# Two blocks of 128 rows taken from the first half of batch 0, in a Fourier mixing and mixture-of-experts kernel

## The chip, the cores and the metric

The kernel runs on one core of one Trainium2 chip. The core has a matrix engine (TensorE, PE in the profile, with its weight loads as PEld), a vector engine (VectorE, DVE), a scalar engine (ScalarE, ACT), GpSimd (POOL), and SyncE (SP), which here only issues transfers. The metric is the device time of one execution in microseconds (us). The kernel before takes 1270.7 us, the median of 3 runs (1270.32 to 1275.03).

## The reference

The input `x` has 8 batches of 2496 rows of 256 values. Each batch goes through a two-dimensional Fourier transform, of which the real part is kept. The 19968 resulting rows are tokens for a layer of 8 experts: the largest of 8 logits chooses a token's expert.

```python
X = np.fft.fft(x, axis=1)
X = np.fft.fft(X, axis=2)
x = X.real                              # (8, 2496, 256) -> (19968, 256)
logits = x @ w_gate                     # 8 experts
expert_idx = np.argmax(logits, axis=1)
gate_w = softmax(logits)[arange(N), expert_idx]
for e in range(8):                      # the rows of expert e
    h = np.maximum(x_e @ w1[e], 0.0)    # 256 -> 1024
    y_e = h @ w2[e]                     # 1024 -> 256
out = gate_w[:, None] * y               # in the tokens' order
```

All arithmetic is in float32. No token is dropped, whatever the experts' loads are.

## The kernel before, in words

**The transform.** A batch is worked in two passes. `first(b)` loads three tiles `xq`, folds them on VectorE (L295 to L306), multiplies them (`s`, TensorE) and writes the result to `Td` in DRAM (L342). `regroup(b, h)` reads `Td` back in another layout into a tile `t4` (t<-Td, L354), one transfer for each half of the batch. `second(b)` makes two more products of it (`pr` and `p`): for each of the two halves h, five windows of 128 positions with two tokens each. A window ends in VectorE's copies into `lg` (the logits, L408) and `rows` (the tokens, L410). After five windows `route(b, h)` finds each token's expert and its place in `Xs`, a buffer in DRAM with one region for each expert, and advances `base`, the next free place of each region. It puts ten scatters (128 rows each) on the list `waiting`. `send()` issues one of them on GpSimd (L236, Xs<-rows,pi). So a batch takes twenty scatters, ten for each half.

**The plans.** `rounds()` says, for each batch, how many blocks of which size can be worked once that batch has been scattered, whatever the experts' loads: blocks that are certain to be full. `plan(b, size, k, last)` computes on VectorE which expert and which rows of `Xs` each of k blocks has, some two dozen small instructions on one partition (L488 to L521) in four stretches with a `yield` behind each. Its tables have MOST = 21 entries, whatever k is. The result lies in `tabs`. `gone` keeps the first row of each region that no plan has given away yet.

**The blocks.** `in_order()` lists all blocks. `experts(todo)` works them. For each block SyncE reads the table, fetches the rows (`fetch_rows`, L534 and L538, xb<-Xs) and the expert's two weight arrays (`fetch_weights`, L544 and L546, 1 MB each, three buffers each). VectorE turns the rows (`turn`, L582) and ScalarE negates half of them (L585); TensorE multiplies (`ph`), VectorE and ScalarE take the positive part (L827, L829), TensorE multiplies again (`py`), ScalarE scales by the gate (L881), and GpSimd scatters the result to the output. Blocks from batch 2's round on have 512 rows, and most use a scheme with seven products in place of eight.

**What sets the order.** Every engine works its instructions in the order in which the program issues them, and the program is written as generators that are stepped in turn. The loop over b at the end takes steps of `experts` for round b - 1 and, for a share of each, steps of `side`: the plans of the round (`close`), the passes of the batches that follow (`mixed`, `ahead_of`), and `send`. In the first round, `experts` waits until the table of its first block exists, asks for its weights, has all waiting scatters issued and waits until the batch counts as whole; then it fetches the rows, lets nine steps of other work go ahead, and turns the first block.

**Which fetch waits for which scatter.** `sent` and `taken` tell the tile framework that a fetch for a block of round b waits for the scatters of batches up to b and not for later ones. Batch 0's two halves have the same number b = 0 there, so the first fetch waits for all twenty scatters of batch 0. The framework has eight semaphores for SyncE's and ScalarE's transfers together, taken in turn: a transfer waits for the one eight places before it. GpSimd's scatters have eight of their own.

**The first round before.** Batch 0 gives two blocks of 256 rows and four of 128 (1024 rows); batch 1 gives four of 256.

Of the kernel before, what the change touches and what calls it, by code (L numbers as in the profile page):

```python
# [15 lines left out]
ALU = mybir.AluOpType  # L16
ACTF = mybir.ActivationFunctionType
AX_X = mybir.AxisListType.X
PSUM = bass.MemoryType.PSUM

B, S, D = 8, 2496, 256
NA, NB = 104, 24
# [9 lines left out]
HW = NW // 2  # L32
HALF = -(-NG // 2)
LAST = NW * 128 - (NG - 1) * GP
NT = B * S
E, F = 8, 1024
FC = F // 128
BIG, BLK, REST = 512, 256, 128
# [12 lines left out]
def bc(ap, axis, n):  # L51
    shape = list(ap.shape)
    shape.insert(axis, n)
    return ap[tuple([slice(None)] * axis + [None])].to_broadcast(shape)
# [72 lines left out]
    return {n: np.ascontiguousarray(v, dtype=np.float32) for n, v in c.items()}  # L127


def rounds():  # L130

    want = [((256, 2), (128, 4)), ((256, 4),)] + [((512, B),)] * (B - 2)
    plan, used = [], 0

    def full(done, size):
        return max(0, -(-(done - used - E * (size - 1)) // size))

    for b in range(B):  # L140
        done = (b + 1) * S
        now = []
        for size, most in want[b]:
            k = min(full(done, size), most)
            if k:
                now.append((size, k, False))
            used += size * k
        if b == B - 1:
            k = full(done, BLK)
            used += BLK * k  # L150
            now.append((BLK, k, False))
            now.append((REST, (NT - used + E * (REST - 1)) // REST, True))
        plan.append(now)
    return plan

SURE = -(-(NT - sum(size * k for now in rounds() for size, k, last in now if not last)) // REST)


def in_order():


    todo = []
    for b, now in enumerate(rounds()):
        parts = [[(b, size, last, i) for i in range(k)] for size, k, last in now]
        if b == B - 1:
            few, many = parts[-2:]
            sure, more = many[:SURE], many[SURE:]
            k = len(few)  # L170
            end = more[(len(more) + 1) // 2:]
            more = more[:len(more) - len(end)]
            rest = []
            for i in range(k):
                rest += few[i:i + 1] + sure[len(sure) * i // k:len(sure) * (i + 1) // k][:1]
                rest += more[i:i + 1]
                rest += sure[len(sure) * i // k:len(sure) * (i + 1) // k][1:]
            parts = parts[:-2] + [rest + end]
        todo += sum(parts, [])
    return todo  # L180
# [5 lines left out]
AHEAD = 12  # L186
WARM = 16
MOST = max(k for now in rounds() for _, k, _ in now)


def halved(b, size):

    return size == 512 and b > 2 or size == 256 and b == B - 1
# [22 lines left out]
def kernel(ctx: ExitStack, tc, x, w_gate, w1, w2, out):  # L216
    nc = tc.nc
    vec, act, pool = nc.vector, nc.scalar, nc.gpsimd
# [50 lines left out]
    con, k = {}, 0  # L269
# [91 lines left out]
    def second(b):  # L361

        t4 = None

        def turn_last(h):

            nonlocal t4
            t4 = ahead.pop((b, "t4", h))
            n = min(HALF, NG - h * HALF)
            pr = pm_.tile([GP, HALF], F32, tag="m", name="pr")  # L370
            mm(pr[:, 0:n], con["rot"][:], t4[0:GP, 0:n, H])
            act.copy(t4[0:GP, 0:n, H], pr[:, 0:n])

        def group(g):
            i, n = g % HALF, LAST if g == NG - 1 else GP
            p2 = pm_.tile([128, 2, n], F32, tag="m", name="p2")
            for c in range(2):
                mm(p2[:, c], t4[0:GP, i, c * H:(c + 1) * H], con["m2"][:, c, 0:n])
            act.copy(zz[:, :, g * GP:g * GP + n], p2[:])
            if g == HALF - 1:  # L380
                turn_last(1)

        def mirror(rows, k):
            act.copy(free(rows[:], (k + 1) * W + D - 1, [-W, 2], [-1, H - 1]),
                     free(rows[:], k * W + 1, [W, 2], [1, H - 1]))

        turn_last(0)
        yield
        group(0)
        yield  # L390
        group(1)
        yield
        for h in range(2):
            rows = sp.tile([128, NSL, W], F32, tag="rows", name="rows")
            lg = sp.tile([128, NSL, E], F32, tag="lg", name="lg")
            for i in range(HW):
                w, k = HW * h + i, 2 * i
                if w + 2 < NG:
                    group(w + 2)
                p3 = pm_.tile([128, 2 * NY + 2 * E + 1], F32, tag="m", name="p3")  # L400
                z = zz[:, :, 128 * w:128 * (w + 1)]
                mm(p3[:, 0:NY + 2 * E], z[:, 0], con["rd"][:, 0, 0:NY + 2 * E], True, False, skip_group_check=True)
                mm(p3[:, NY:], z[:, 1], con["rd"][:, 1], False, True, skip_group_check=True)
                zs = sp.tile([128, NY + 1], F32, tag="zs", name="zs")
                act.copy(zs[:], p3[:, NY + 2 * E:])  # L405
                if i:
                    mirror(rows, k - 2)
                vec.tensor_copy(lg[:, k:k + 2], p3[:, NY:NY + 2 * E].rearrange("p (m e) -> p m e", m=2))  # L408
                for m, op in enumerate((ALU.add, ALU.subtract)):
                    vec.scalar_tensor_tensor(rows[:, k + m, 0:NY], p3[:, 0:NY], zs[:, 0:1], zs[:, 1:],  # L410
                                             op0=ALU.add, op1=op)
                yield
            mirror(rows, k)
            yield from route(b, h, rows, lg)

    def route(b, h, rows, lg):
# [6 lines left out]
        mx, eq, v = small("mx", NSL), small("eq", NSL, E), small("v", NSL)  # L423
# [31 lines left out]
        vec.tensor_tensor(nxt[:], rk[:, NSL], base[:], op=ALU.add)  # L455
        base = nxt
        for s in range(NSL):
            waiting.append((b, pf[:, s:s + 1], pi[:, s:s + 1], rows[:, s]))

    waiting = deque()  # L460

    def send():

        if waiting:
            b, place, idx, rows = waiting.popleft()
            if b:
                due = sp.tile([128, 1], F32, tag="due", name="due", bufs=8)
                act.copy(due[:], place)  # L468
                pool.tensor_copy(idx, due[:])  # L469
            sent(put_row(Xs, idx, rows, E * CAP - 1, "xs"), b)  # L470
# [7 lines left out]
    def plan(b, size, k, last):  # L478
# [3 lines left out]
        def one(name, *dims, dt=F32):  # L482
            return cp.tile([1, *dims], dt, tag="p_" + name, name="p_" + name, bufs=2 if name == "gone" else 1)
# [10 lines left out]
        vec.tensor_tensor(ex[:], ce[:], nb[:], op=ALU.subtract)  # L494
        yield
        vec.scalar_tensor_tensor(rb[:], ex[:], -float(size), gone[:], op0=ALU.mult, op1=ALU.add)
        ge, ei = one("ge", MOST, E), one("ei", MOST)
        val, eq, rw = one("val", MOST, E + 1), one("eq", MOST, E + 1), one("rw", MOST)
        vec.tensor_tensor(ge[:], bc(bk["i"], 2, E), bc(ce[:], 1, MOST), op=ALU.is_ge)
        vec.reduce_sum(ei[:], ge[:], axis=AX_X)  # L500
        yield
        vec.tensor_tensor(eq[:], bc(ei[:], 2, E + 1), bc(bk["e9"], 1, MOST), op=ALU.is_equal)
        vec.memset(val[:, :, E:E + 1], float(E * CAP))
        vec.scalar_tensor_tensor(val[:, :, 0:E], bc(bk["i"], 2, E), float(size), bc(rb[:], 1, MOST),
                                 op0=ALU.mult, op1=ALU.add)
        yield
        vec.tensor_tensor(val[:], val[:], eq[:], op=ALU.mult)
        vec.reduce_sum(rw[:], val[:], axis=AX_X)
        tab = cp.tile([1, 2, MOST], I32, tag="p_tab", name="p_tab", bufs=4)
        vec.tensor_copy(tab[:, 0], rw[:])  # L510
        vec.tensor_scalar(tab[:, 1], ei[:], E - 1.0, None, op0=ALU.min)
        if last:
            cnt = cp.tile([1, 1], I32, name="cnt")
            vec.tensor_copy(cnt[:], ce[:, E - 1:E])
# [213 lines left out]
    def experts(todo):  # L728
# [35 lines left out]
        for k, (b, size, last, at) in enumerate(todo):  # L764
            n, m = size // 128, BIG // size
            if not k:
                while todo[0][:3] not in tabs:
                    yield 0, False
                fetch_some(0, 1)
                while b not in whole:  # L770
                    yield 0, True
                fetch_some(0)
                for _ in range(9):
                    yield 0, False
                for xT in turn(b, size, xbs[0][0]):
                    pass
# [129 lines left out]

    def close(b):

        for size, k, last in rounds()[b]:
            yield from plan(b, size, k, last)  # L910

    def through(b):
# [5 lines left out]
    def ahead_of(b):  # L918

        yield from first(b)  # L920
        regroup(b, 0)
        regroup(b, 1)
# [43 lines left out]
    for c in range(2):  # L966
# [6 lines left out]
            vec.tensor_scalar(con["rd"][:, c, to + E:to + 2 * E], pg[:], con["sgn"][:], None, op0=ALU.mult)  # L973
        else:
            vec.tensor_copy(con["rd"][:, c, to + E:to + 2 * E], pg[:])
    early = ahead_of(1)
    for _ in range(7):
        next(early)
    for k, _ in enumerate(second(0)):
# [5 lines left out]
    for b in range(1, B):  # L985
# [3 lines left out]
        ticks = TICKS + AHEAD * (b == 1)  # L989
        if b == 1:  # L990
            side = woven(chain(close(0), through(0)), chain(early, side))
        blocks = [(size, k * size / BIG, halved(b - 1, size)) for size, k, _ in rounds()[b - 1]]
        total = sum(k * (15 if seven_ else 16) for _, k, seven_ in blocks)
        open_ = sum(k * (8 if seven_ else 16) for _, k, seven_ in blocks)
        while done < total:
# [73 lines left out]
```

## Time and profile before

| | |
|---|---|
| median of 3 runs | 1270.7 us (1270.32 to 1275.03) |
| profiled execution | 1270.37 us, span 1268.5 us, mean TensorE clock 0.98 |
| TensorE | 1212.5 us busy (96% of the span), weight loads 1083.6 us |
| VectorE, ScalarE, GpSimd | 773.6, 421.5 and 445.7 us busy |
| DMA | 249.79 MB, mean 197 GB/s; SyncE's queue holds 49.9% of sixteen engines' span |
| weight transfers | 132 of 1 MB, 7.0 us from issue to landing (median) |
| rows for blocks | 112 transfers of 128 KB, 52 of 64 KB, 100 of 32 KB |

A line of the timeline gives the start, the duration, the engine, the line of the program, the operation, the tiles written and read (out<-in), the shapes, how many records, and in brackets the engine's idle time before it with what ended it. Most matrix products have line L221 and most GpSimd transfers L236, since helpers issue them; they are told apart by their tiles. A float32 product shows as two records. The page's line PEclk gives, for 40 equal slices of the span, the clock that TensorE was granted, in tenths. A line of the waits gives who waited for whom, the sum in us, how often, and the longest.

### The profile page before, as it was taken

What the parts mean: (1) busy time and instruction counts of PE and PEld (TensorE: products, weight loads), DVE (VectorE), ACT (ScalarE), POOL (GpSimd) and SP (SyncE); (2) the same over time, 40 slices, a digit from 0 to 9 for tenths busy, and PEclk for the clock granted to TensorE, in tenths of its full rate; (3) what the DMA queues carried; (4) which work ended last, traced back from release to release, by engine and by line L of the source; (5) the groups of instructions that cost most, each with busy time, mean ns of one, the idle gap of its engine ahead of it and who ended that gap; (6) DMA issues with size and microseconds to landing.
All of it is one profiled execution on the core that took longest, in us unless ns stands there. A gap on an engine that the chain in (4) does not pass through costs nothing.

```text
span 1268.5 us, 22212 instructions
## 1 busy us (share of the span) xinstructions
PE 1212.5 (96%) x7289; PEld 1083.6 (85%) x7289; DVE 773.6 (61%) x1884; ACT 421.5 (33%) x1087; POOL 445.7 (35%) x527
## 2 busy tenths in 40 slices
PE   5759999999999999999999999999999999999996
PEld 4548987876788899888998999889999999999995
DVE  4546334443465788576866588686788884444662
ACT  1423332332243433434243433432332322222222
POOL 0145427145116522472226612561462331111112
PEclk9869999999999999999999999999999999999997
DMA  8769898765348454573336435443444348777786
GB/s 239 246 194 334 306 311 305 193 223 176 124 151 254 139 148 154 165 249 114 101 127 207 136 117 171 133 153 96 146 130 159 104 157 288 278 284 270 270 292 231
DMA packets 163216, 249.79 MB, mean 197 GB/s; under 512 B 118601, under 2 KB 130227, under 8 KB 143516
## 3 DMA queue, kind: packets, MB, share of 16 engines
q1 hardware_dynamic: 146327, 203.28, 49.9%
q0 software_dynamic: 15888, 42.14, 9.2%
q10 hardware_dynamic: 885, 2.94, 0.7%
q8 instruction: 59, 0.97, 0.3%
q14 instruction: 57, 0.47, 0.1%
HBM read 194.91 MB, written 54.83 MB: 197 GB/s over the span
## 4 chain that ended last, share of the span: by engine, by line
PE 71%; issue 16%; DMA 4%; POOL 4%; DVE 3%; ACT 0%; POOLq 0%; SPq 0%; DVEq 0%; ACTq 0%
PE py L221 19%; PE a L221 10%; PE c L221 10%; PE d L221 7%; PE ph L221 6%; PE p L221 6%; PE b L221 5%; PE e L221 3%; PE s L221 3%; POOL out_dram L236 3%; DMA xq<-in_x_dram 1%; POOL Xs L236 1%; DMA t<-Td 1%; DMA w<-c_w 1%; DMA Xs<-rows,pi 0%
## 5 line engine op out<-in xcount | busy, mean ns | idle before, releaser
L236 POOL DMA_INDIRECT out_dram<-y,ro x163 | 161.0, 988 | 633.8 <-ACT y L678 297.9
L221 PE MATMUL py<-w_sb,hT 128*128 128x256 f32 x1504 | 340.3, 380 | 0.0
L221 PEld LDWEIGHTS py<-w_sb,hT 128*128 128x128 f32 x1504 | 282.0, 191 | 36.1 <-issue 1.0
L236 POOL DMA_INDIRECT Xs<-rows,pi x160 | 163.7, 1023 | 113.7 <-DVE rows L410 55.0
L221 PE MATMUL ph<-xT,w_sb 128*128 128x128 f32 (+2 forms) x992 | 173.0, 331 | 9.8 <-DVE ro L782 8.7
L221 PEld LDWEIGHTS ph<-xT,w_sb 128*128 128x128 f32 x992 | 137.7, 194 | 34.2 <-issue 16.5
L221 PE MATMUL a<-xT,w_sb 128*128 128x256 f32 (+1 forms) x512 | 118.1, 358 | 0.3 <-DVE xT L582 0.2
L827 DVE TENSOR_SCALAR hT<-ph 128x512 f32<-128x512 f32 x43 | 29.7, 690 | 127.7 <-PE ph L221 68.9
L585 ACT ACTIVATE xT<-xT 128x256 f32<-128x256 f32 (+1 forms) x94 | 36.5, 388 | 185.8 <-DVE xT L582 135.7
L221 PEld LDWEIGHTS a<-xT,w_sb 128*128 128x128 f32 x512 | 88.6, 191 | 10.6 <-DVE xT L582 1.3
L881 ACT ACTIVATE y<-py,xb 128x256 f32<-128x256 f32 x97 | 45.8, 473 | 154.4 <-PE py L221 152.6
L634 DVE TENSOR_TENSOR hT<-hT,b 128x512 f32<-128x512 f32 x57 | 39.2, 688 | 80.6 <-PE b L221 53.9
L408 DVE COPY lg<-p 128x16 f32<-128x16 f32 x80 | 13.8, 172 | 113.8 <-ACT zs L405 113.7
L644 ACT ACTIVATE hT<-a 128x512 f32<-128x512 f32 x57 | 34.0, 597 | 140.2 <-PE a L221 140.2
L221 PE MATMUL s<-xq,w 104*112 104x256 f32 (+2 forms) x208 | 61.5, 420 | 11.6 <-DVE xq L297 8.9
L582 DVE STREAM_TRANSPOSE xT<-xb 128x512 f32<-128x512 f32 (+1 forms) x94 | 58.7, 627 | 12.7 <-DMA xb<-Xs 12.7
L469 POOL CAST pi<-due 128x1 int32<-128x1 f32 x140 | 42.2, 301 | 68.8 <-ACT due L468 68.7
L221 PE MATMUL a<-w_sb,hT 128*128 128x128 f32 x528 | 66.0, 276 | 0.0
L221 PE MATMUL p<-table,zz 128*128 128x145 f32 (+1 forms) x320 | 58.3, 308 | 8.0 <-DVE rows L410 6.6
L221 PE MATMUL d<-w_sb,hT 128*128 128x128 f32 x528 | 65.5, 275 | 0.0
L221 PEld LDWEIGHTS a<-w_sb,hT 128*128 128x128 f32 x528 | 63.2, 192 | 0.7
L221 PEld LDWEIGHTS d<-w_sb,hT 128*128 128x128 f32 x528 | 62.2, 192 | 0.0
(144 smaller groups left out, 2086.0 us busy)
## 6 DMA issues: line engine op xcount, KB each, us to landing
w_sb<-in_moe_w_dram SPq DMA_DIRECT2D x132, 1024.0 KB, 7.0
xq<-in_x_dram SPq DMA_DIRECT2D x24, 896.0 KB, 8.6
xb<-Xs SPq DMA_DIRECT2D x112, 128.0 KB, 3.3
Td<-t SPq DMA_DIRECT2D x18, 448.0 KB, 3.3
t<-Td SPq DMA_DIRECT2D x8, 768.0 KB, 9.5
t<-Td SPq DMA_DIRECT2D x8, 640.0 KB, 9.2
xb<-Xs SPq DMA_DIRECT2D x52, 64.0 KB, 5.9
xb<-Xs SPq DMA_DIRECT2D x100, 32.0 KB, 5.4
```

What stands on the lines that cost most here:

```text
L221: nc.tensor.matmul(o, lhsT=lhsT, rhs=rhs, start=start, stop=stop, **kw)
L236: return unordered(pool.indirect_dma_start(out=dst, out_offset=bass.IndirectOffsetOnAxis(ap=idx, axis=0), in_=rows, in_offset=None, bounds ...
L408: vec.tensor_copy(lg[:, k:k + 2], p3[:, NY:NY + 2 * E].rearrange("p (m e) -> p m e", m=2))
L469: pool.tensor_copy(idx, due[:])
L582: vec.transpose(free(xT[:], 256 * h, [32, n // 32], [BIG, 2], [1, 32]), free(xb, 512 * h, [64, n // 32], [1, 2], [2, 32]))
L585: act.activation(odd, odd, ACTF.Copy, scale=-1.0)
L634: vec.tensor_tensor(h12, h11, b[:], op=add)
L644: act.activation(h11, a[:], ACTF.Relu)
L827: vec.tensor_scalar(o, ph[:], 0.0, None, op0=ALU.max)
L881: act.activation(y[:, i % 2], py[:], ACTF.Copy, scale=meta[:, i, 1:2])
```

## The change

Batch 0's first half gets a round of its own, with the number -1. Its 1256 tokens are certain to fill two blocks of 128 rows (`HEAD`). Their plan, `close(-1)`, is stepped in `second(0)` once in each window of the second half, so that it uses `base` as the first half leaves it. The first half's scatters are marked -1, so the fetch of these two blocks waits for the ten scatters of the first half alone. The remaining rounds take the rows given away into account: batch 0's own round then has one block of 256 and four of 128 (with the head 1024 rows again, in seven blocks in place of six). The tables of all plans are cut to the k entries that the plan needs. In `experts`, fifteen steps of other work go ahead of the first block's turning instead of nine.

```diff
--- before.py
+++ after.py
@@ -127,12 +127,15 @@
     return {n: np.ascontiguousarray(v, dtype=np.float32) for n, v in c.items()}
 
 
+HEAD = [(REST, -(-(2 * 128 * HW - NB - E * (REST - 1)) // REST), False)]
+
+
 def rounds():
 
 
 
     want = [((256, 2), (128, 4)), ((256, 4),)] + [((512, B),)] * (B - 2)
-    plan, used = [], 0
+    plan, used = [], sum(size * k for size, k, _ in HEAD)
 
     def full(done, size):
         return max(0, -(-(done - used - E * (size - 1)) // size))
@@ -154,15 +157,20 @@
     return plan
 
 
-
-SURE = -(-(NT - sum(size * k for now in rounds() for size, k, last in now if not last)) // REST)
+def stage(b):
+    return HEAD if b < 0 else rounds()[b]
+
+
+
+SURE = -(-(NT - sum(size * k for now in [HEAD, *rounds()] for size, k, last in now if not last)) // REST)
 
 
 def in_order():
 
 
     todo = []
-    for b, now in enumerate(rounds()):
+    for b in range(-1, B):
+        now = stage(b)
         parts = [[(b, size, last, i) for i in range(k)] for size, k, last in now]
         if b == B - 1:
             few, many = parts[-2:]
@@ -394,6 +402,8 @@
             rows = sp.tile([128, NSL, W], F32, tag="rows", name="rows")
             lg = sp.tile([128, NSL, E], F32, tag="lg", name="lg")
             for i in range(HW):
+                if h and not b:
+                    next(heads, None)
                 w, k = HW * h + i, 2 * i
                 if w + 2 < NG:
                     group(w + 2)
@@ -455,7 +465,7 @@
         vec.tensor_tensor(nxt[:], rk[:, NSL], base[:], op=ALU.add)
         base = nxt
         for s in range(NSL):
-            waiting.append((b, pf[:, s:s + 1], pi[:, s:s + 1], rows[:, s]))
+            waiting.append((b if b or h else -1, pf[:, s:s + 1], pi[:, s:s + 1], rows[:, s]))
 
     waiting = deque()
 
@@ -463,7 +473,7 @@
 
         if waiting:
             b, place, idx, rows = waiting.popleft()
-            if b:
+            if b > 0:
                 due = sp.tile([128, 1], F32, tag="due", name="due", bufs=8)
                 act.copy(due[:], place)
                 pool.tensor_copy(idx, due[:])
@@ -494,21 +504,22 @@
         vec.tensor_tensor(ex[:], ce[:], nb[:], op=ALU.subtract)
         yield
         vec.scalar_tensor_tensor(rb[:], ex[:], -float(size), gone[:], op0=ALU.mult, op1=ALU.add)
-        ge, ei = one("ge", MOST, E), one("ei", MOST)
-        val, eq, rw = one("val", MOST, E + 1), one("eq", MOST, E + 1), one("rw", MOST)
-        vec.tensor_tensor(ge[:], bc(bk["i"], 2, E), bc(ce[:], 1, MOST), op=ALU.is_ge)
-        vec.reduce_sum(ei[:], ge[:], axis=AX_X)
-        yield
-        vec.tensor_tensor(eq[:], bc(ei[:], 2, E + 1), bc(bk["e9"], 1, MOST), op=ALU.is_equal)
+        ge, val, eq = (one(name, MOST, E + 1)[:, 0:k] for name in ("ge", "val", "eq"))
+        ei, rw = (one(name, MOST)[:, 0:k] for name in ("ei", "rw"))
+        count = bk["i"][:, 0:k]
+        vec.tensor_tensor(ge[:, :, 0:E], bc(count, 2, E), bc(ce[:], 1, k), op=ALU.is_ge)
+        vec.reduce_sum(ei, ge[:, :, 0:E], axis=AX_X)
+        yield
+        vec.tensor_tensor(eq, bc(ei, 2, E + 1), bc(bk["e9"], 1, k), op=ALU.is_equal)
         vec.memset(val[:, :, E:E + 1], float(E * CAP))
-        vec.scalar_tensor_tensor(val[:, :, 0:E], bc(bk["i"], 2, E), float(size), bc(rb[:], 1, MOST),
+        vec.scalar_tensor_tensor(val[:, :, 0:E], bc(count, 2, E), float(size), bc(rb[:], 1, k),
                                  op0=ALU.mult, op1=ALU.add)
         yield
-        vec.tensor_tensor(val[:], val[:], eq[:], op=ALU.mult)
-        vec.reduce_sum(rw[:], val[:], axis=AX_X)
+        vec.tensor_tensor(val, val, eq, op=ALU.mult)
+        vec.reduce_sum(rw, val, axis=AX_X)
         tab = cp.tile([1, 2, MOST], I32, tag="p_tab", name="p_tab", bufs=4)
-        vec.tensor_copy(tab[:, 0], rw[:])
-        vec.tensor_scalar(tab[:, 1], ei[:], E - 1.0, None, op0=ALU.min)
+        vec.tensor_copy(tab[:, 0, 0:k], rw)
+        vec.tensor_scalar(tab[:, 1, 0:k], ei, E - 1.0, None, op0=ALU.min)
         if last:
             cnt = cp.tile([1, 1], I32, name="cnt")
             vec.tensor_copy(cnt[:], ce[:, E - 1:E])
@@ -770,7 +781,7 @@
                 while b not in whole:
                     yield 0, True
                 fetch_some(0)
-                for _ in range(9):
+                for _ in range(15):
                     yield 0, False
                 for xT in turn(b, size, xbs[0][0]):
                     pass
@@ -906,7 +917,7 @@
 
     def close(b):
 
-        for size, k, last in rounds()[b]:
+        for size, k, last in stage(b):
             yield from plan(b, size, k, last)
 
     def through(b):
@@ -973,7 +984,7 @@
             vec.tensor_scalar(con["rd"][:, c, to + E:to + 2 * E], pg[:], con["sgn"][:], None, op0=ALU.mult)
         else:
             vec.tensor_copy(con["rd"][:, c, to + E:to + 2 * E], pg[:])
-    early = ahead_of(1)
+    heads, early = close(-1), ahead_of(1)
     for _ in range(7):
         next(early)
     for k, _ in enumerate(second(0)):
@@ -989,7 +1000,7 @@
         ticks = TICKS + AHEAD * (b == 1)
         if b == 1:
             side = woven(chain(close(0), through(0)), chain(early, side))
-        blocks = [(size, k * size / BIG, halved(b - 1, size)) for size, k, _ in rounds()[b - 1]]
+        blocks = [(size, k * size / BIG, halved(b - 1, size)) for size, k, _ in (HEAD if b == 1 else []) + stage(b - 1)]
         total = sum(k * (15 if seven_ else 16) for _, k, seven_ in blocks)
         open_ = sum(k * (8 if seven_ else 16) for _, k, seven_ in blocks)
         while done < total:
```

## The prediction

> **What bounds the kernel now.** I read the busy shares first, then TensorE's waits, then the order of time around the one long wait, then DMA by stage.
>
> ```profile
> PE 1212.5 (96%) x7289; PEld 1083.6 (85%) x7289; DVE 773.6 (61%) x1884; ACT 421.5 (33%) x1087; POOL 445.7 (35%) x527
> PEclk9869999999999999999999999999999999999997
> ...
> PE ph L221 <- DVE ro L782: 8.7, 1, 8.7
> PE pr L221 <- DMA t<-Td: 2.8, 2, 2.4
> ```
>
> TensorE is busy 96% of 1268.5 us, so only its holes can be won. The waits of the first 130 us show one hole of 8.7 us: the first expert product `ph`. From 130 to 345 us the list has a single wait over 1 us, 3.2 us of `pr` on t<-Td. The chain of waits tells what the long hole consists of (start, us, what):
>
> ```profile
> 81.81 0.31 issue
> 82.12 2.42 DMA Xs<-rows,pi
> 84.79 0.35 SPq L534
> 86.39 1.92 DMA xb<-Xs
> 88.44 0.71 DVE xT L582
> 89.21 3.77 PE ph L221 x8
> ```
>
> The twentieth scatter of batch 0 lands at 84.5; only then are the rows fetched (84.79), turned (88.44) and multiplied (89.2). TensorE had nothing from 80.5:
>
> ```profile
> 77.94 1.21 PE L221 MATMUL p<-table,t 120*128 120x120 f32 x4 [0.20 <-DVE rows L410]
> 78.94 0.41 PE L221 MATMUL pr<-t,table 120*120 120x5 f32 x2
> 79.21 1.32 PE L221 MATMUL p<-table,zz 128*128 128x145 f32 x4
> 89.20 3.78 PE L221 MATMUL ph<-xT,w_sb 128*128 128x256 f32 x8 [8.67 <-DVE ro L782]
> ...
> 131.87 0.28 PE L221 MATMUL pr<-t,table 120*120 120x6 f32 x2
> ```
>
> The last line is the place where I expect the gain to be cut: batch 2's first product from `t`, which runs without a wait now. Its transfer landed 5 us before (issued 118.52, 8.3 us to landing: 126.8). DMA by stage (start:end, PE, PEld, DVE, ACT, POOL busy, clock, DMA share, GB/s):
>
> ```profile
> 60.00:80.00 20.00, 12.42 (x62) 10.69 (x62) 17.29 (x73) 5.28 (x17) 15.73 (x15) 0.69 0.77 271
> 80.00:90.00 10.00, 1.33 (x5) 0.89 (x4) 1.45 (x5) 0.99 (x3) 2.48 (x3) 0.50 0.32 81
> 90.00:110.00 20.00, 19.99 (x107) 17.25 (x106) 10.16 (x39) 7.42 (x23) 3.52 (x7) 0.87 0.92 301
> 110.00:130.00 20.00, 18.83 (x103) 16.29 (x102) 13.94 (x52) 6.96 (x30) 16.30 (x24) 1.00 1.01 326
> ```
>
> In the hole DMA idles too (0.32); right behind it DMA is full (0.92, 1.01). So two resources stand close together there.
>
> **The Trainium skill.** "TensorE: Matmul & The Clock Gate", "What's actually happening", says that the array falls to half clock after an idle window of about 3.4 us and is released after about as long of work. The trace agrees: clock 0.50 from 75 to 95 us, the first eight `ph` take 3.78 us where later ones take 1.89. "DMA: Bandwidth & Descriptors", "Queues, rings and completion order", says that one queue's descriptors are consumed in ring order on each DMA engine, and the queues are served in turn. The trace fits: rows issued at 94.6 behind a 0.9 MB `xq` took 10.0 us to land (1.9 us without it).
>
> **The change, part by part.**
>
> *Head plan (21 small DVE instructions, L488 to L521).* A plan takes 4.0 us in the trace (from 70.19: 1.4 + 0.7 + 0.5 + 1.4). At 2 entries instead of 21, six instructions fall from 0.32-0.34 to about 0.16 (the 1x8 rows): 3.0 us. The two plans of batch 0 shorten likewise, by 1.0 and 0.9. Net +1.1 us, against 1.8 us of DVE gaps between 54.5 and 59.6. DVE is full from 59.6 to 77.1; the first head block is turned behind the same work: at 77 to 78. POOL is covered: the second half's indices come up to 2 us later than 63.3, and POOL gets to them at 69.2. The other plans save about 9 us of DVE in all, off the path: nothing.
>
> *Head rows.* In the built program their fetch waits for exactly ten scatters. The tenth starts at 67.37; scatters land in 2.4 to 3.2 us here, 4.7 to 6.5 in full stretches: 70 to 73.5. First issue to data took 3.65 us (84.79 to 88.44): 74 to 77, just ahead of DVE. First `ph` at 78.0 (transposition 0.43, the copy into `ro`).
>
> *Fifteen steps.* They put the plans and folds on DVE ahead of the transposition. On TensorE only the `s` of 68.2 stands ahead of the first `ph` in the built order; two rounds of `p`, an `s` and a `pr` that run from 69.2 to 80.5 now come behind it. So TensorE will stand still from about 70 to 78, a hole of 7 to 9 us for DVE. It takes the place of two: 3.48 us at 71 (for `rows`) and the 8.67 us.
>
> *Two blocks of 128 for one of 256.* TensorE: 2 x 3.57 (32 records of 128x128) against 6.91, +0.23 us; `py` is the same 3.46 per 128 rows. One weight pair more, 2.1 MB, and this counts below.
>
> *TensorE up to `pr`.* From 69.17 to 131.87 are 62.7 us; less waits 3.48 + 8.67 + 1.17 + 0.4, and half clock 2.9 (74.7 to 80.5) and 3.0 (89.2 to 94.6), 43.1 us at full clock. Adding up the groups gives 41.5; I take 42.5, with the 0.23. The restart at 78 is cold once: 2.5; small waits 0.5. So `pr` is reached at 123.5 (121.5 to 125.5), 8.4 us earlier.
>
> *The queue on SP up to `pr`.* In the built order two things move: the weights of the second and third block stand ahead, and t<-Td of batch 2 stands behind the rows and weights of block (0,128,1), not before them. Each transfer also waits for the eighth before it, so t<-Td waits for the `xq` just before it. Prices from 99.8 to 126.8 us: 2.25 us per MB, rows of 256 2.0, rows of 128 1.2, a scatter or output 0.37. From 79.7: two weight pairs 9.4, Td and xq 3.1, rows 3.2, four scatters 1.5: 96.9. Then a weight pair, Td and xq 7.8; batch 1's scatters run beside it, one per 1.45 us, a quarter of the engines: 10.5, to 107.4. The last Td can't start before its `s`, about 109.5. Then Td and xq 3.1, rows 1.2, a weight pair 4.7, the first t<-Td 1.8: 10.8, with scatters 14.5, an output and first latency 2: 126. Five weight pairs stand ahead, three now; the idle 77 to 91 pays for most of it.
>
> *So `pr` waits* 126 - 123.5 = 2.5 us, which it doesn't now. Under about 3.4 us the clock holds; over it a restart costs 1.9 (after 3.15 us idle at 211, `p` took 1.19 for 0.6, `ph` x8 3.13 for 1.89). I take 0.5 of it. Sum: 126 + 0.5 - 131.87 = -5.4 us.
>
> *What is late next.* The weights of the following blocks are issued when buffers come free; (0,128,2)'s pair lands near 133 and is needed near 149. From there order and amounts on every engine are those of now, so the shift stays. The tail has the same count of blocks. Without DMA's idle stretch t<-Td would land 8 us later, and the change would lose.
>
> The profiled execution took 1270.4 (1268.5 and 1.9 around it), its neighbours 1270.3 to 1275.0, median 1270.7. 1270.4 - 5.4 = 1265.0.
>
> **Rivals.** *TensorE's whole lead stays:* if t<-Td lands before 123.5, 1270.4 - 8.4 = 1262. For it: single stretches of 5 us reach 404 GB/s, where my price is nearer 370. Against it: five weight pairs, and the late `s`. *Slower, through the same transfer:* from a landing at 130.0 on, the cold restart (1.9) makes it slower than now. For it: one `xq` took 12.1 us and one weight 11.1 in full stretches, and both stand ahead in series. At 134 it is 1274.5. Against it: the idle stretch is really free. *It doesn't do what it says:* the head's rows or its transposition come 8 us late, at 86, TensorE stands still until then with its `p` work queued behind, and 2.1 MB more follow: 1271 to 1277. Against it: ten counted scatters, and DVE's order.
>
> **How the numbers follow.** Forecast 0.52 (own range 1262.5 to 1269), the whole lead 0.25, slower through t<-Td 0.17, not doing what it says 0.06. About 0.5% (6.4 us) is what a measurement of this kernel can tell from no change. Faster, under 1264.3: 0.23 of the second case and 0.17 of the first, 0.40. Slower, over 1277: 0.05 and 0.03, 0.08. Same 0.52. The range 1259.5 to 1274.5 leaves out a tenth on each side.
>
> **What would show it.** Right: the first `ph` starts at 77 to 80 behind a wait of 7 to 9 us that DVE ends; a new wait of 1 to 5 us at the third `pr`, released by t<-Td, at 122 to 129; DMA share near 1 from 80 on; the same work behind it, about 5 us earlier. Wrong: first `ph` after 82 (then a late scatter or row fetch is named there), no wait at `pr` (the whole lead), or `pr` after 130.

## The result and the profile after

The changed kernel takes 1282.65 us (median of 11 runs, 1279.65 to 1292.63), the kernel before beside it 1273.59 us (11 runs, 1270.32 to 1279.32). The ratio is 1.0069, with a 95% interval of 1.0051 to 1.0087: slower, where 1265.0 us was forecast, 5.4 us under the profiled execution of the kernel before. The profiled execution of the changed kernel took 1284.77 us, its span is 1283.0 us. The two profiled executions lie 14.4 us apart, the two medians 9.1, so differences between these two traces are somewhat larger than the loss.

The page of the changed kernel first, the lines for busy time and for TensorE's clock in 40 slices:

```profile
PE 1215.7 (95%) x7321; PEld 1086.5 (85%) x7321; DVE 767.0 (60%) x1906; ACT 421.7 (33%) x1088; POOL 442.0 (34%) x527
PEclk9978899899999999999999999999999999999998
```

TensorE has 3.2 us more work than before and 14.5 us more span, so most of the loss is waiting. TensorE's waits of the first 160 us (us in all, times, longest):

```profile
PE pr L229 <- DMA t<-Td: 7.7, 2, 7.2
PE ph L229 <- DVE ro L793: 7.3, 1, 7.3
PE rk L229 <- DVE oh L441: 4.8, 3, 3.1
PE p L229 <- ACT t L380: 4.6, 1, 4.6
```

The hole ahead of the first `ph` is 7.3 us in place of 8.7. Three others are new: `pr` on t<-Td (7.2), `rk` on `oh` (3.1), and a `p` behind a standstill at 63 us (4.6). The chain of waits of the changed kernel (start, us, what) runs through the head's rows and then through the transfer:

```profile
74.42 3.49 DMA Xs<-rows,pi
...
81.29 0.45 DVE xT L593
81.79 3.61 PE ph L229 x16
...
127.47 1.63 issue
129.10 12.34 DMA t<-Td
141.49 0.57 PE pr L229 x2
```

The same places in TensorE's timeline of the changed kernel (`rk`, a part of `route`, ranks the tokens of each expert):

```profile
81.79 3.61 PE L229 MATMUL ph<-xT,w_sb 128*128 128x128 f32 x16 [7.27 <-DVE ro L793]
...
99.71 0.25 PE L229 MATMUL rk<-oh,tri 128*128 128x88 bf16 x1 [3.06 <-DVE oh L441]
100.21 3.76 PE L229 MATMUL ph<-xT,w_sb 128*128 128x128 f32 x16
...
141.49 0.57 PE L229 MATMUL pr<-t,table 120*120 120x6 f32 x2 [7.17 <-DMA t<-Td]
```

TensorE reached the third `pr` at 134.3 (141.49 less 7.17) and began it at 141.49; the kernel before began it at 131.87. (Third as the forecast counts, from 60 us on.) From there on the two traces keep their distance: the `pr` of 214.28 us comes at 226.06, 11.8 later, the last one 13.4 later (741.51 against 728.07). So most of the loss is made before that `pr`, with batch 0's and batch 1's blocks. DMA by stage, in the windows that were shown of the kernel before (start:end, then PE, PEld, DVE, ACT, POOL busy, clock, DMA share, GB/s):

```profile
60.00:80.00 20.00, 6.09 (x33) 5.10 (x32) 14.10 (x64) 2.83 (x9) 12.90 (x13) 0.62 0.74 260
80.00:90.00 10.00, 8.21 (x54) 8.06 (x55) 3.52 (x18) 2.77 (x9) 2.80 (x3) 0.74 1.00 363
90.00:110.00 20.00, 16.71 (x105) 15.37 (x104) 9.08 (x40) 7.22 (x22) 2.54 (x5) 0.83 0.89 278
110.00:130.00 20.00, 18.41 (x105) 15.72 (x104) 10.93 (x53) 7.23 (x30) 13.96 (x24) 1.00 0.73 206
```

Between 60 and 80 us TensorE works 6.1 us where it worked 12.4. And the DMA engines, which the forecast had near full from 80 us on, are at 0.73 in the stage before `pr`, where they were at 1.01: SyncE issued no transfer from 107.7 to 119.2 us.

### The profile page after: what moved, and what is told of

The parts are those of the page before. It is cut to its first block, busy times and chain, and to the rows that moved or that the text cites. A ratio compares the mean times of both kernels' runs of the same rounds, so it can differ in the third digit from the quotient of the medians.

```text
span 1283.0 us, 22338 instructions
## 1 busy us (share of the span) xinstructions
PE 1215.7 (95%) x7321; PEld 1086.5 (85%) x7321; DVE 767.0 (60%) x1906; ACT 421.7 (33%) x1088; POOL 442.0 (34%) x527
## 4 chain that ended last, share of the span: by engine, by line
PE 67%; issue 19%; POOL 5%; DMA 3%; DVE 3%; ACT 1%; SPq 0%; POOLq 0%; another core or an unknown queue 0%; DVEq 0%; ACTq 0%
PE py L229 18%; PE a L229 10%; PE c L229 10%; PE d L229 6%; PE ph L229 6%; PE p L229 6%; PE b L229 5%; PE e L229 3%; POOL out_dram L244 3%; PE s L229 3%; POOL Xs L244 1%; DMA w<-c_w 1%; DMA t<-Td 1%; DMA xq<-in_x_dram 1%; DVE xq L303 0%
## 5 line engine op out<-in xcount | busy, mean ns | idle before, releaser
L244 POOL DMA_INDIRECT Xs<-rows,pi x160 | 161.0, 1006 | 116.2 <-DVE p_nb L501 53.2
L229 PE MATMUL ph<-xT,w_sb 128*128 128x128 f32 (+2 forms) x1024 | 176.9, 330 | 7.9 <-DVE ro L793 7.3
L229 PEld LDWEIGHTS ph<-xT,w_sb 128*128 128x128 f32 x1024 | 142.5, 199 | 31.1 <-issue 16.5
L229 PEld LDWEIGHTS p<-table,t 120*128 120x128 f32 x352 | 55.3, 208 | 13.7 <-ACT t L380 6.8
L229 PE MATMUL p<-table,t 120*128 120x120 f32 (+1 forms) x352 | 57.8, 291 | 6.2 <-ACT t L380 6.2
```

Source lines behind the costliest of these rows:

```text
L229: nc.tensor.matmul(o, lhsT=lhsT, rhs=rhs, start=start, stop=stop, **kw)
L244: return unordered(pool.indirect_dma_start(out=dst, out_offset=bass.IndirectOffsetOnAxis(ap=idx, axis=0), in_=rows, in_offset=None, bounds ...
```

## The experiments

Each group of runs was made on one chip at one time and is compared with runs of the kernel before in between, whose median lay between 1264.9 and 1283.4 us in the five groups.

**First theories.** One: the head's first pair of weights, asked for at 58.7 us right behind t<-Td of batch 1, delays that transfer and makes the standstill at 63 us. Two: the order on SyncE, with t<-Td of batch 2 behind the rows and weights of block (0,128,1). In both the shorter plans cost nothing.

*The shorter plans alone.* The kernel before, with this for all plans and nothing else:

```diff
-        ge, ei = one("ge", MOST, E), one("ei", MOST)
-        val, eq, rw = one("val", MOST, E + 1), one("eq", MOST, E + 1), one("rw", MOST)
+        ge, val, eq = (one(name, MOST, E + 1)[:, 0:k] for name in ("ge", "val", "eq"))
+        ei, rw = (one(name, MOST)[:, 0:k] for name in ("ei", "rw"))
...
```

> The shorter block plans alone, on the kernel before: no head blocks, nine steps. Both theories (loss through the order of SyncE's queue; loss that begins with the early weight pair) say the plans are innocent: about 9 us less VectorE work, nearly all off the path, ratio to before 0.998 to 1.001. If the ratio is above 1.004, the plans are part of the loss and both theories are incomplete.

Measured: 1290.62 us against 1283.44, ratio 1.0065 (1.0044 to 1.0086). Neither theory had that. `hT` is the activation that a block's second product reads. In its timeline TensorE waits 2.1 to 2.9 us near 421, 571 and 720 us for `hT` of a seven-product block, one of them thus:

```profile
417.65 1.03 PE L221 MATMUL e<-xs,w_sb 128*128 128x256 f32 x4
421.52 1.35 PE L221 MATMUL c<-xT,ws 128*128 128x256 f32 x4 [2.85 <-DVE hT L641]
422.66 1.91 PE L221 MATMUL a<-xT,w_sb 128*128 128x256 f32 x4
```

The traces before and after the change have no such waits. The same kernel was run again later, on another chip.

*t<-Td of batch 2 ahead of the next rows and weights.* The changed kernel with

```diff
-            fetch_some(k)
+            fetch_some(k, 2 if k == 2 else 3)
```

> The change, with t<-Td of batch 2 issued before the rows and weights of block (0,128,1), as the kernel before has it. Queue theory: t<-Td lands about 6 us earlier, the wait of 7.2 us at the third pr falls under 3 us and the half clock behind it goes too; 7 to 9 us less than the change, about level with before (ratio 0.998 to 1.002). Early-pair theory: the standstill of VectorE and ScalarE at 63 to 68 us is still there and the first ph still starts near 82; the time falls by less than 4 us.

Measured: 1293.02 us, ratio 1.0070 (1.0049 to 1.0092). The wait of `pr` is gone, the time is not:

```profile
137.43 0.28 PE L229 MATMUL pr<-t,table 120*120 120x6 f32 x2
...
149.52 1.21 PE L229 MATMUL p<-table,t 120*128 120x120 f32 x4 [5.01 <-ACT zz L387]
```

t<-Td was issued at 125.56 and TensorE came to `pr` at 137.4; the rows and weights behind it went out at 129.25 to 137.20 and a `p` waited 5.0 us, 12 us later. ScalarE and VectorE stood still ahead of it, as at 63 us, and the trace names only "remote" (another core or an unknown queue) as what released them. Whether those rows and weights had to do with it isn't shown. The hole ahead of the first `ph` (7.26 us) and the wait of `rk` (3.06 us) are still there. At its eighth `pr` the trace stands at 334.44 us, against 326.76 for the plans alone and 326.20 for the run with an unread pair of weights below, two kernels of this group without the head. So moving the order on the queue did not win the head's loss back in this trace, whose execution (1300.13 us) is the slowest of its twelve. The ratio itself says little. This kernel has the short plans, which cost 0.65% in this group, and its trace has the late waits for hT too (2.1 to 2.9 us, four times). Theory two falls as the whole cause; that the order is worth a part isn't excluded.

*The head's weights behind its rows.* The changed kernel without the early request:

```diff
-                fetch_some(0, 1)
                 while b not in whole:
```

> The change, with the first head block's weights issued behind its rows (near 74 us) instead of ahead of them (58.7). Early-pair theory: no engine stands still for over 3 us at 60 to 69, the first ph starts at 78 to 81 (its weights then land at 80 to 81), and the time falls by 2 to 4 us. Queue theory: the standstill has another cause and stays, first ph near 82 or later, the time within 1.5 us of the change's or above it.

Measured: 1295.34 us, ratio 1.0098 (1.0065 to 1.0131), and the standstill is the same, a `p` at 69.65 behind 4.64 us. Here too the ratio holds the late waits for hT (three of 2.8 us).

*An unread pair of weights in the kernel before.* One pair of 1 MB arrays asked for right behind t<-Td of batch 1, and read by nothing:

```diff
+    e1_sb = bp.tile([128, 2, F], F32, tag="w1", name="e1_sb", bufs=3)
+    nc.sync.dma_start(out=e1_sb[:], in_=w1[0:1].rearrange("o p c f -> p (o c) f"))
...
```

> The kernel before, with one more pair of 1 MB weight loads issued right behind t<-Td of batch 1 (near 59 us), which nothing reads. Early-pair theory: VectorE and ScalarE stand still for 3 to 5 us at 62 to 68 in this kernel too, and it is 2 to 5 us slower than before. Queue theory: no such standstill; the pair lies in a stretch with room, the time within 1.5 us of before.

Measured: 1284.07 us, ratio 1.0006 (0.9988 to 1.0023). 2.1 MB more at that place cost nothing. With the standstill there without the early weights, and no time lost with them, theory one falls.

**Where the parts lie.** The next four, on another chip, take the change apart.

> The kernel before, unchanged, traced on the same chip as the kernels beside it. If the waits of TensorE for hT of 2 to 3 us near 421, 571 and 720 us, which the runs of short plans showed, come from the short plans, this trace has none of them or at most the one of 1.6 us that the run with an early pair of weights had. If they come from the chip, it has three or four of them. Span expected 1276 to 1286 us.

Measured: 1277.56 us; no wait of TensorE for hT in any of the three places.

> The changed kernel, unchanged, on the same chip. If the head and the plans lose in different places, its trace is about 10 us behind that of the kernel before at the pr of 226 us, and loses another 3 to 5 us in each of the rounds with short plans at 421, 571 and 720 us: ratio 1.009 to 1.015. If the loss is made once, in the head, ratio 1.006 to 1.008, and no such waits.

Measured: 1283.40 us, ratio 1.0065 (1.0040 to 1.0090), none of those waits either; the third `pr` at 139.81, behind 7.44 us. The loss is made once, in the head.

The changed kernel with the plans of the kernel before (the first diff the other way round):

> The change with whole-length plans: the two blocks of 128 rows, the early start and the fifteen steps stay, each plan works all its columns again. If the short plans carry the loss, 0.996 to 1.001. If the head loses about 10 us by itself, 1.005 to 1.009. The forecast on record put the head at 5 us faster, 0.996.

Measured: 1285.13 us, ratio 1.0070 (1.0050 to 1.0090). The head carries the whole loss here, whatever the plans.

The kernel before with short plans for blocks of 512 rows alone:

```diff
+        m = k if size == BIG else MOST
+        ge, val, eq = (one(name, MOST, E + 1)[:, 0:m] for name in ("ge", "val", "eq"))
...
```

> The kernel before with short plans for the blocks of 512 rows alone (five columns in place of twenty-one); the plans of the blocks of 256 and 128 rows stay whole. If the loss of the short plans is made where the 512-row plans run (the waits for hT near 421, 571 and 720 us), 1.003 to 1.007. If it is made in the first 160 us, by the plans of the first two batches, 0.999 to 1.001.

Measured: 1274.89 us against 1275.76, ratio 0.9993 (0.9982 to 1.0004). The shorter plans of the seven-product rounds cost nothing here.

**New theories.** Three: the first half's early transfers collide with t<-Td of batch 1. Four: blocks of 128 rows use up the three pairs of weight buffers with half the work and starve the DMA engines. Five: the place of the head in TensorE's order: fifteen steps leave TensorE a hole, and all of batch 2's transform behind it comes late.

The kernel before with fifteen steps:

```diff
-                for _ in range(9):
+                for _ in range(15):
```

> The kernel before with fifteen steps of other work ahead of its first block in place of nine, and nothing else. If the order of TensorE's work alone costs (the first block of 256 rows starts some 10 us later in TensorE's order), 1.002 to 1.006. If steps in front only fill the hole of 6 to 9 us ahead of the first ph, 0.994 to 0.999.

Measured: 1269.37 us against 1266.89, ratio 1.0023 (1.0010 to 1.0035). There the first `ph` waits 1.8 us, so the hole is filled, and still 2.5 us are lost: the order has a price of its own.

The changed kernel with its head waiting for all twenty scatters:

```diff
-            waiting.append((b if b or h else -1, pf[:, s:s + 1], pi[:, s:s + 1], rows[:, s]))
+            waiting.append((b or -1, pf[:, s:s + 1], pi[:, s:s + 1], rows[:, s]))
```

> The change with the head rows waiting for all twenty scatters of batch 0, as the kernel before does, in place of the first half's ten; two blocks of 128 rows and fifteen steps stay. If the early transfers collide with t<-Td of batch 1 and that is the loss, 0.998 to 1.002. If the two half-size blocks cost (three pairs of weights cover 512 rows in place of 768, and 2.1 MB more), it stays at 1.005 to 1.010.

Measured: 1282.88 us, ratio 1.0127 (1.0096 to 1.0157): about twice the loss. The first `ph` waits 17.7 us:

```profile
65.85 2.02 PE L229 MATMUL s<-xq,w 104*112 104x256 f32 x4 [0.36 <-PE p L229]
85.58 3.79 PE L229 MATMUL ph<-xT,w_sb 128*128 128x128 f32 x16 [17.71 <-DVE xT L593]
```

So the early start is worth time; theory three falls. The lines also show how little the fifteen steps put ahead of the first `ph` on TensorE: one `s` is the last of it. In the program the steps take from the plans of batch 0 (`close(0)`) too, of which the kernel before has the first behind it when its nine begin, since its first table comes from that plan.

The changed kernel with more steps, `range(20)` and `range(26)` in place of `range(15)`:

> The change with twenty steps in front in place of fifteen: p, zz and s groups up to the next pr now stand ahead of the first ph of the head. If the loss is the hole of 6 to 7 us ahead of that ph and the late Td it makes (the third pr then waits 7 us for t<-Td), the wait ahead of ph falls under 3 us, Td comes 4 to 6 us sooner, ratio 0.998 to 1.003. If the loss is the split into blocks of 128 rows, it stays at 1.005 to 1.009.

Measured: 1264.64 us, ratio 0.9992 (0.9976 to 1.0008). The third `pr` starts at 123.25, without a wait.

> The change with twenty-six steps in front: nearly all of batch 2's p, zz and s stand ahead of the first ph. If the late Td is the loss, the third pr no longer waits, 0.995 to 1.002. If the split is the loss, the head's DMA is starved all the same and it stays at 1.005 or above.

Measured: 1266.22 us, ratio 0.9991 (0.9981 to 1.0002), third `pr` at 117.77 without a wait. The loss is gone with the two blocks of 128 rows, their weights and the short plans all in place. Theory four falls; five stands. In both traces t<-Td of batch 2 also goes out ahead of the next rows and weights (113.66 before 115.51 us, 106.67 before 109.63).

**What was still open: chips, plans, and how many steps.** Four more on a further chip.

> The kernel before, unchanged, traced beside the three runs below on one chip. On a chip where the transfers of the head land early, its third pr comes at about 128 to 132 us with no wait of TensorE over 4 us at 62 to 75 us, as in the trace before the change; on a chip where they land late, at about 137 us.

Measured: 1267.11 us (one execution), third `pr` at 130.50:

```profile
97.97 0.21 PE L221 MATMUL rk<-oh,tri 128*128 128x88 bf16 x1 [0.20 <-DVE oh L431]
...
130.50 0.28 PE L221 MATMUL pr<-t,table 120*120 120x6 f32 x2
```

> The changed kernel, unchanged. If fifteen steps are too few wherever it runs, 1.005 to 1.009 again, with the third pr waiting 6 to 8 us for t<-Td. If the loss comes only where the transfers of 58 to 70 us land late, 0.998 to 1.003 on a chip where the standstill of 4 to 5 us near 63 us is missing.

Measured: 1272.83 us against 1264.90, ratio 1.0052 (1.0032 to 1.0073). In this trace the standstill at 63 us is missing, and the loss is there all the same. So that standstill, whatever makes it, isn't the main cause, and this trace is the clean one to read:

```profile
66.53 2.02 PE L229 MATMUL s<-xq,w 104*112 104x256 f32 x4
76.00 3.44 PE L229 MATMUL ph<-xT,w_sb 128*128 128x128 f32 x16 [7.46 <-DVE ro L793]
...
89.16 0.67 PE L229 MATMUL p<-table,zz 128*128 128x145 f32 x4
89.66 1.03 PE L229 MATMUL s<-xq,w 104*112 104x256 f32 x4
93.75 0.25 PE L229 MATMUL rk<-oh,tri 128*128 128x88 bf16 x1 [3.06 <-DVE oh L441]
...
94.25 3.76 PE L229 MATMUL ph<-xT,w_sb 128*128 128x128 f32 x16
...
133.36 0.57 PE L229 MATMUL pr<-t,table 120*120 120x6 f32 x2 [6.80 <-DMA t<-Td]
```

> The kernel before with the short plans alone, once more. If the short plans themselves cost, 1.004 to 1.008 again. If what it lost came from the waits for hT at 421, 571 and 720 us of that one chip, 0.998 to 1.001 here, with no such waits in its trace.

Measured: 1262.54 us, ratio 0.9982 (0.9968 to 0.9996), with none of the waits at 421, 571 and 720 us. The short plans don't cost; what they lost before belongs to that one group of runs (more below).

> The change with eighteen steps in front: the first ph of the head then stands behind the same pr, p and zz of batch 1 as the first ph of the kernel before does with its nine. If the loss is the hole of 7 us that fifteen steps leave and all that it makes late, most of it is gone: 0.998 to 1.003, the third pr at 124 to 130 us. If it needs all of twenty steps for another reason (the last Td ahead of the head's second block), it stays at 1.004 to 1.008.

Measured: 1258.82 us, ratio 0.9948 (0.9931 to 0.9965): faster than both kernels, by about what had been forecast for fifteen steps (0.9957), though by another way than forecast: there a hole of 7 to 9 us was part of the sum. Its TensorE timeline at the same places:

```profile
72.57 0.77 PE L229 MATMUL p<-table,zz 128*128 128x145 f32 x4 [1.78 <-DVE rows L420]
73.26 1.93 PE L229 MATMUL s<-xq,w 104*112 104x256 f32 x4
...
79.72 3.79 PE L229 MATMUL ph<-xT,w_sb 128*128 128x128 f32 x16 [1.49 <-DVE ro L793]
...
87.07 3.62 PE L229 MATMUL py<-w_sb,hT 128*128 128x256 f32 x16
90.52 0.20 PE L229 MATMUL rk<-oh,tri 128*128 128x88 bf16 x1
...
120.50 0.29 PE L229 MATMUL pr<-t,table 120*120 120x6 f32 x2
```

Three more steps put two groups of `p` and `zz`, an `s` and a third group with the second `pr` ahead of the head. They fill the hole: 7.46 us become 1.78, 1.49 and some 0.9. They also change what stands between the last `p` that the routing needs and `rk`: a `ph`, an `s` and a `py` (84.42 to 90.52 us) in place of one `s`. Behind these VectorE's routing is done in time: 3.06 us become nothing, and the restart at half clock that follows (`ph` 3.76 us for 1.95) is gone. They bring batch 2's `s`, and so its last Td, forward. SyncE's transfers with fifteen steps:

```profile
113.11 0.31 SPq L350 DMA_DIRECT2D Td<-t  x1
...
115.73 2.79 SPq L545 DMA_DIRECT2D xb<-Xs  x4
...
120.39 0.33 SPq L557 DMA_DIRECT2D w_sb<-in_moe_w_dram  x1
122.53 2.40 SPq L362 DMA_DIRECT2D t<-Td  x2
```

and with eighteen:

```profile
105.39 0.34 SPq L350 DMA_DIRECT2D Td<-t  x1
114.28 1.81 SPq L362 DMA_DIRECT2D t<-Td  x2
116.94 2.22 SPq L545 DMA_DIRECT2D xb<-Xs  x4
```

The last Td goes out 7.7 us sooner, t<-Td stands ahead of the next rows and weights again, and is there 6.2 us after its issue at the latest, in place of 10.8. TensorE's waits from 62.5 us to the third `pr` add up to 17.96 us with fifteen steps (7.46, 3.06, 0.22, 0.42, 6.80) and to 4.33 with eighteen (0.45, 1.78, 0.44, 1.49, 0.17): 13.6 us less, against 12.9 between the two starts of `pr` and 14.0 between the two medians. DMA by stage of this kernel shows the starved stage filled (95 to 125 us; the changed kernel on the same chip has 0.90 and 271 GB/s there):

```profile
95.00:125.00 30.00, 29.65 (x181) 26.15 (x180) 16.28 (x64) 11.47 (x46) 22.91 (x36) 1.00 1.02 361
```

Two last runs, under the chip number of the second group, at another time:

> The change with eighteen steps once more, on whichever chip it lands. If its gain is the hole that fifteen steps leave and the waits that follow from it, 0.993 to 0.997 again, third pr near 121 us without a wait. If it was a lucky order on that one chip, 0.998 to 1.003.

Measured: 1260.75 us against 1266.24, ratio 0.9962 (0.9943 to 0.9981), third `pr` at 120.66 without a wait. The gain holds on a second chip.

> The change with seventeen steps: the first group of ph stands two p and zz groups and an s later than with fifteen, but still ahead of the pr, p and zz that end batch 1's first read. If what counts is TensorE's hole ahead of the first ph, the hole is about half that of fifteen steps and the ratio lies between, 0.996 to 1.002. If it takes all of the pr group ahead of the head, it stays at 1.003 to 1.007.

Measured: 1260.87 us, ratio 0.9954 (0.9935 to 0.9973). The first `ph` starts at 76.20 behind 1.04 us, `pr` at 121.08 behind 1.70 us. Seventeen is as good as eighteen, so it doesn't take the `pr` group ahead of the head: two groups of `p` and `zz` and an `s` are enough. `rk` doesn't wait there either, and t<-Td goes out ahead of the next rows and weights (114.26 before 116.08 us). Sixteen was not run. With twenty and more the head itself comes late (first `ph` at 84.89 behind 4.30 us, and at 94.92) and the gain is spent again. TensorE's waits from 62.5 us to the third `pr` add up to 9.2 us in both traces, against 4.3 and 5.9 in the two with eighteen steps. And although the third `pr` is early there, the fifth is not: 210.18 and 209.51 us, against 203.37 and 203.80.

**What these runs do not separate.** Seventeen steps and more change three things at once: the hole ahead of the head, the wait of `rk`, and the order of t<-Td on SyncE's queue. That the place of the head in the order of work makes the loss is shown, since moving it alone takes the loss away. How much of it each of the three makes is read from the traces, not from a run that changes one of them in a group where nothing else costs.

## Why the prediction was wrong, point by point

*What bounds the kernel* was right: only the holes of the first 160 us moved.

*Head plan* and *Head rows* held where no standstill comes between: first `ph` at 76.0 in the clean trace, 78.0 in the forecast. In the first trace after it came at 81.8. There VectorE and ScalarE stand still from 63.3 to 68.1. It goes by the group of runs: all four traces of the change and its variants in the first two groups have it (the kernel before took 1283.4 and 1275.8 us there), the seven in the later ones, at 1264.9 to 1266.9 us, do not. With the early weights put later it stayed, and early weights in the kernel before cost no time. It stays open, and it is not needed for the loss.

*Fifteen steps* was read rightly: one `s` ahead of the first `ph` and a hole of 7 to 9 us, measured 7.3 and 7.5. That the plans' shortening is worth nothing off the path also held in two groups (0.9993 for the blocks of 512 rows, 0.9982 for all); in a third it cost 0.65%, with waits that the other groups don't have.

*TensorE up to `pr`* is the first step that failed. The work was right: from 76.00 to 126.56, TensorE's 46.85 us of records, less some 4.1 us for two restarts at half clock, leave 42.7 us, forecast 42.5. What was mis-sized was "small waits 0.5". With the head pulled ahead, only an `s` of 1.0 us stands between the last `p` that the routing needs and `rk`, which waits 3.06 us for VectorE's routing; the kernel before covers that to 0.2 us. The clock doesn't outlast it: the `ph` behind takes 3.76 us in place of 1.95, and the next `p` and `zz` 0.8 more. That is 5.7 us, and only one restart was counted. The Trainium skill ("TensorE: Matmul & The Clock Gate", "What's actually happening") gives an idle window of about 3.4 us, on which the forecast built its "under about 3.4 us the clock holds"; here 3.06 us were followed by half clock. The measurement decides. The forecast had the same thing in its own trace: the half clock that it priced came behind 3.15 us. So TensorE comes to `pr` at 126.6 in the clean trace, not at 123.5, although the head began 2 us sooner than forecast, and at 134.3 in the first one, with the standstill besides.

*The queue on SP up to `pr`* is the second step that failed. The last Td was to go out at 109.5; it went at 113.1 and, in the first trace, at 119.2, since its `s` stands behind that same `rk`. From there to the start of `pr` 16.5 us were forecast; 20.2 and 22.3 were measured. The two orders that the step rests on were read rightly (five pairs of weights, t<-Td behind rows and weights of (0,128,1)), and so was the direction. The price behind the 16.5 us was too low: from 113 to 133 us of the clean trace the DMA engines were full (0.99) and moved 333 GB/s, where the forecast calls its price "nearer 370". (That doesn't fit its own 2.25 us per MB either, which are 444 GB/s for a transfer alone.)

*So `pr` waits 2.5 us* became 6.8 and 7.2, with a restart of its own (in the clean trace the `ph` behind it takes 3.55 us for 1.95), for which the forecast took 0.5 us. Both terms are late for one reason: the last Td and TensorE's arrival hang on the same `s` and `rk`, but from that Td on the transfer takes 20.2 us more, and TensorE comes to `pr` after 13.5. Counted against the kernel before on the same chip, `pr` begins 2.9 us later (133.36 against 130.50) instead of 5.4 earlier, and by the `pr` of 229 us it is 5.7 later.

*What is late next:* the shift does stay from about 230 us on (5.7 us in every later `pr` of the clean pair).

The rival that came true is *slower, through the same transfer*: from a landing at 130 on it decides, and 134 would give 1274.5. The clean trace landed at about 133 and took 1273.28. That the time fits so well is luck, since the kernel before took 1267.11 us beside it and not 1270.4: by its sum a landing at 133 costs some 3 us, and 6.2 were lost. The first trace lies beyond it. *TensorE's whole lead* of 8.4 us is there only once the hole is filled with work, as with eighteen steps on the same chip (third `pr` 10.0 us earlier). *It doesn't do what it says* fell: the head does start early, and making it wait costs about as much again (1.0127).

## What to carry to other kernels

Pulling a block of work ahead is worth what the work behind it loses: write the order on the waiting engine down to the next product that feeds a transfer, and check each product that was covered by a longer one before. When two chains meet at one wait, TensorE's own and a transfer that TensorE feeds, a delay ahead of both is paid in both. And before such a change is given up, move its place by a few steps: fifteen steps were 0.5 to 0.7% slower, seventeen and eighteen 0.4 to 0.5% faster, with the same work.

## What the runs showed of the hardware

Groups of runs differ in where they wait, and not only by a common factor. In the first group, three kernels with short plans (the plans alone and two variants of the change) had waits of 2 to 3 us for hT in the rounds of seven-product blocks (near 421, 571 and 720 us with the plans alone), and VectorE and ScalarE there started about 2 us behind the recorded ends of the products that they wait for; one with whole plans had 1.65 us at 421 and 2.65 at 852. No trace of the other groups has them, with short plans or long. The kernel before was not traced in that group, so what makes them is open. They put the plans alone at 0.65% slower there, and the same kernel was 0.18% faster elsewhere. Even under one chip number the median of the kernel before was 1275.8 us in one group and 1266.2 in another. So half a per cent can be read only between runs of one group, and, as the plans alone show, is better seen in a second group too.

An idle time of 3.06 us was enough for half clock: in the changed kernel `ph` takes 3.76 us behind such a wait and 1.95 us elsewhere. With eighteen steps a wait of 1.78 us was followed by it: the `p` before the wait ran at full clock (70.18 us, 0.60), the `s` at 73.26, behind the wait and 0.7 us of work, took 1.93 us for 1.03. In the second run of that kernel the same `s` took 1.12 us behind a wait of 2.78 us. So in these traces no single length of a wait divides full clock from half.
